# Ordering the loads of q, k and v behind earlier transposes in the DMA queue of a fused attention and mixture-of-experts kernel

## The chip, the cores and the metric

The kernel runs on one core of a Trainium2 chip. The metric is the device time of one launch in microseconds. The core has five engines that run their own instruction streams in order: TensorE (PE, with its weight loads PEld), VectorE (DVE), ScalarE (ACT), GpSimd (POOL) and SyncE (SP). SyncE computes nothing here; it issues nearly all DMAs, one after the other.

## The reference, cut to what matters

Bucketed attention (a query sees the keys whose six sign bits equal its own), then a two-layer feed-forward net, then a mixture of eight experts, of which each token uses two.

```python
q_bits = (einsum('bhsd,dk->bhsk', q, proj) > 0); k_bits = ...   # batch 2, heads 8, seq 768, dim 64
mask = q_bucket[:, :, :, None] == k_bucket[:, :, None, :]
scores = where(mask, scale * q @ k.T, -1e9)
attn_out = softmax(scores) @ v
x = attn_out as [1536, 512]
h = x @ w_in;  x = (h * sigmoid(1.702 * h)) @ w_out              # d_ff 2048
...
out[mask] += top2_w[mask, k, None] * (relu(x[mask] @ w1[e]) @ w2[e])   # 8 experts, top 2
```

## The kernel before

Everything is computed with pairs of half-precision numbers (a high and a low part), so a float32 input is loaded, converted, split and laid out before TensorE can use it.

**The steps.** The attention runs in 96 steps g: batch b, chunk cc of 256 queries, pair of heads hp, head h and half t. A step makes the scores (`qk`, L254), the row maximum (`rowmax`, L266 on VectorE), the exponential (`expo`, L275 on ScalarE), its split (`e_hi` L314, `e_lo` L321 or L323), and from step 16 on a DMA transpose of the result (`et<-er`, L327). `pv` (L368) multiplies with v after two heads. Before step 0 there are 17 steps with negative numbers, in which the first tiles are made ready. From step 20 on the first feed-forward net runs in between, chunk by chunk (`moe_pe`: L460 and L471; L478, L490, L504, L505 around them), and the routing of its tokens. After step 100 come the rest of that net and the experts (L799, L821).

**The preparation of q and k.** `load` (L118) issues the load of a q tile (128 KB) or a k or v tile (192 KB). A tile goes through `stack_hi` two steps later (L144 on VectorE or GpSimd, L145 on GpSimd, L151), `stack_lo` (L158 on ScalarE and then the transpose L169), `buckets` and `one_hot` (L179 to L203) and `stack_end` (L210 on ScalarE and then the transpose L211). Loads of k and v share four buffers (tag x32); a buffer is free when the tile in it has been split, for v by `v_hi` (L230, L231 on ScalarE) and `v_lo` (L237 on GpSimd). v tiles of the first 16 steps take another way (`v_load32`, L221).

**The weights of the first net.** `w_load` (L417) loads 32 blocks of 512 KB into three buffers; `w_bits` makes three passes over a block on VectorE (L428, L431, L434), `w_split` scales and splits it on ScalarE and GpSimd (L444 or L442, L445, L446). A buffer is free after L446.

**What sets the order.** The program hands over each step's calls in lists (`at` late in the step, `soon` and `start` earlier), and tables say in which step a tile is loaded, two steps ahead of `stack_hi`. For steps below 100 (`GM=100`) the order is not the program's: a scheduler lays the instructions out engine by engine, by its own model of time, and may put an instruction far ahead of its step as soon as its inputs and its buffer are free in that model. A load has no inputs. From step 100 on the written order holds. On the chip every engine, SyncE too, takes its instructions strictly in the order that results.

Of the kernel before, what the change touches and what calls it, by code (L numbers as in the profile page):

```python
# [60 lines left out]
def fused(ctx: ExitStack, tc: tile.TileContext, q, k, v, proj, w_in, w_out, w_gate, w_noise, noise,  # L61
          w1, w2, out, dbg=None):
    nc = tc.nc
# [48 lines left out]


    raw, rows, kts, qts, vts, bks = {}, {}, {}, {}, {}, {}
    FL = "p h c d -> p (h c) d"


    def load(nm, b, u):  # L118
        hp, i = u
        if nm == "q":  # L120
            x = att.tile([128, 2, CT, D], F32, name="q32")
            PARAM['LE'](nc).dma_start(x.rearrange("p h c d -> p h (c d)"), q[b, 2 * hp:2 * hp + 2].rearrange(
                "h (p c) d -> p h (c d)", c=NT)[:, :, i * CT * D:(i + 1) * CT * D])
        else:
            x = att.tile([128, 1, NT, D], F32, name=f"{nm}32", tag="x32", bufs=4)
            PARAM['LE'](nc).dma_start(x[:, 0].rearrange("p c d -> p (c d)"), (k if nm == "k" else v)[b, 2 * hp + i].rearrange(
                "(p c) d -> p (c d)", c=NT))
        raw[nm, b, u] = x

    def stack_hi(nm, b, u):  # L130
# [10 lines left out]
        h0 = 0 if nm == "q" else 64  # L141
        hi = sb[:, :, :, 0:64].rearrange(FL)
        eng = nc.gpsimd if PARAM["HE"](nm, b) == "P" else nc.vector
        eng.tensor_scalar(hi, x.rearrange(FL), GX, GX, op0=OP.add, op1=OP.subtract)  # L144
        nc.gpsimd.tensor_tensor(x.rearrange(FL), x.rearrange(FL), hi, op=OP.subtract)  # L145
        yield
        m, o = PARAM["SC"](nm, b), sa[:, :, :, h0:h0 + 64].rearrange(FL)
        if m == "A":
# [4 lines left out]
    def stack_lo(nm, b, u):  # L153
        x = raw.pop((nm, b, u))
        sa, sb = rows[nm, b, u]
        hp, i = u
        h0 = 64 if nm == "q" else 0
        nc.scalar.activation(sa[:, :, :, h0:h0 + 64].rearrange(FL), x.rearrange(FL), AF.Copy, scale=SH)  # L158
        if nm == "q":
            xt = att.tile([128, 2, 2, CT, 128], F16, name="qt", bufs=3)  # L160
            qts[b, hp, i] = xt
        elif i == 0:
            xt = att.tile([128, 2, 2, NT, 128], F16, name="kt", bufs=4)
            kts[b, hp] = xt
        else:
            xt = kts[b, hp]
        dst = xt if nm == "q" else xt[:, :, i:i + 1]
        rows[nm, b, u] = sb, dst
        nc.sync.dma_start_transpose(dst[:, 0].rearrange("p h c t -> p (h c) t"), sa.rearrange("p h c d -> p (h c d)"))  # L169

    def buckets(nm, b, u):
        sb, xt = rows[nm, b, u]
# [33 lines left out]
    def stack_end(nm, b, u):  # L206
        sb, xt = rows.pop((nm, b, u))
        oh = sb[:, :, :, 64:].rearrange(FL)
        if PARAM["OE"](nm, b) == "D":
            nc.scalar.activation(oh, oh, AF.Identity, scale=BIG, bias=-BIG if nm == "k" else 0.0)  # L210
        nc.sync.dma_start_transpose(xt[:, 1].rearrange("p h c t -> p (h c) t"), sb.rearrange("p h c d -> p (h c d)"))  # L211

    FU = PARAM["FU"]
    vfs = {}
# [25 lines left out]
    st, ets, xts, pos, sms = {}, {}, {}, {}, {}  # L240
# [75 lines left out]
    def e_lo(g):  # L316
        b, cc, hp, h, t = where(g)
        d = st.pop(g)
        er = d["er"]
        if g < NG:  # L320
            (nc.gpsimd if PARAM["LO"](g) else nc.vector).tensor_tensor(er[:, 1], d["e"], er[:, 0], op=OP.subtract)  # L321
        else:
            nc.vector.scalar_tensor_tensor(er[:, 1], d["e"], d["mx"][:, 3:4], er[:, 0], op0=OP.mult, op1=OP.subtract)  # L323
        if t == 0:
            et = att.tile([128, 2 * NT, CT, 128], F16, name="et", bufs=3)
            ets[b, cc, hp, h] = et
        nc.sync.dma_start_transpose(ets[b, cc, hp, h][:, :, t, :], er.rearrange("p s c -> p (s c)"))  # L327

    def early_unit(b, cc, hp):
        return (b * NCH + cc) * 16 + 4 * hp < NG  # L330
# [556 lines left out]
    for b in range(B):  # L887
        for hp in range(HP):
            g = b * NCH * 16 + 4 * hp
# [9 lines left out]
        for cc in range(NCH):  # L899
            for hp in range(HP):  # L900
                g = (b * NCH + cc) * 16 + 4 * hp
# [56 lines left out]
    order = ExitStack()  # L958
    g_lo = min(todo)
    for g in range(g_lo, G1 + 1):  # L960
        if g == max(PARAM["GM"], g_lo):
            order.enter_context(tc.manual_schedule(engines={
                mybir.EngineType.PE, mybir.EngineType.DVE, mybir.EngineType.Activation,
                mybir.EngineType.Pool, mybir.EngineType.SP}))
        if g == NU + 3:
            att_ctx.close()
            m2 = ctx.enter_context(tc.tile_pool(name="m2", bufs=2))
        prev = steps.get(g - 1, [])
        if 0 <= g + 2 < NU:
            qk(g + 2)  # L970
        for f, a in early.pop(g, []):
            f(*a)
        for x in prev:
            moe_act(*x)
        if 0 <= g + 1 < NU:
            rowmax(g + 1)
            expo(g + 1)
            e_hi(g + 1)
        for f, a in first.pop(g, []):
            f(*a)  # L980
        for x in prev:
            moe_dve(*x)
        if 0 <= g < FU:
            e_turn(g)
            e_copy(g)
        elif FU <= g < NU:
            e_lo(g)
        for x in steps.get(g, []):
            moe_pe(*x)
        for x in prev:  # L990
            moe_split(*x)
        by_turns(todo.pop(g, []))
# [52 lines left out]
    with tc.If(most > CAP):  # L1045
        with tc.tile_pool(name="ov", bufs=1) as ov:
# [13 lines left out]
            with tc.For_i(0, E, 1) as e:  # L1060
# [5 lines left out]
                with tc.If(here > CAP):  # L1066
# [12 lines left out]
                    with tc.For_i(0, (OV + 127) // 128, 1) as k_:  # L1079
                        with tc.If(here > k_ * 128 + CAP):  # L1080
# [11 lines left out]
                            xt = rowt.bitcast(F16)  # L1092
# [59 lines left out]
```

## Time and profile before

| | us |
|---|---|
| median of 3 runs (823.86 to 825.7) | 825.37 |
| the profiled execution | 823.72 |
| its span, first to last instruction | 822.0 |
| TensorE busy | 715.9 (87%) |
| VectorE busy | 533.9 (65%) |
| ScalarE busy | 445.0 (54%) |
| GpSimd busy | 267.9 (33%) |

A share over the whole span says little here, since the stages have different limits: the tables of busy time by stretch, the list of waits of an engine and the timeline of SyncE's queue say more. In such a list a wait is put down to what ended last. L12 means line 12 of the kernel; tile names stand as written<-read.

### The profile page before, as it was taken

How to read it: one execution, taken by the hardware profiler on the slowest of the kernel's cores; microseconds unless marked ns; L12 is line 12 of the kernel's file. 1: busy time of each engine (PE TensorE's matmuls, PEld its weight loads, DVE VectorE, ACT ScalarE, POOL GpSimd, SP SyncE). 2: the span in 40 equal slices, each digit the busy share in tenths (PEclk: the TensorE clock that was granted, in tenths of full speed). 3: DMA queues.
4: the chain of work that ended last, by engine and by line, in shares of the span. 5: the costliest groups of instructions: out<-in, count | busy, mean ns of one | idle time of the engine just before them, and what ended most of it. 6: DMA issues, size and time to landing. Idle time of an engine off the chain costs nothing.

```text
span 822.0 us, 14816 instructions
## 1 busy us (share of the span) xinstructions
PE 715.9 (87%) x5398; PEld 446.0 (54%) x5399; DVE 533.9 (65%) x1330; ACT 445.0 (54%) x859; POOL 267.9 (33%) x303
## 2 busy tenths in 40 slices
PE   1676478988988888898999999879999999999995
PEld 1343345646754665466568576547554655556553
DVE  8998799997896789569869526454633525345210
ACT  3778767766765686467567425234533534334220
POOL 6444646560444055314212132241021120311212
PEclk9878789999999999999999999999999999999998
DMA  8999689999999999995797542856875858677213
GB/s 218 224 251 212 180 187 184 255 277 218 175 171 195 154 200 192 225 159 106 119 176 123 102 156 88 221 146 180 250 158 173 199 111 232 135 194 176 28 19 47
DMA packets 268126, 140.04 MB, mean 170 GB/s; under 512 B 224720, under 2 KB 243856, under 8 KB 268048
## 3 DMA queue, kind: packets, MB, share of 16 engines
q1 hardware_dynamic: 261520, 125.37, 68.1%
q0 software_dynamic: 6528, 13.68, 9.3%
q8 instruction: 43, 0.70, 0.4%
q14 instruction: 35, 0.29, 0.1%
HBM read 61.48 MB, written 23.79 MB: 104 GB/s over the span
## 4 chain that ended last, share of the span: by engine, by line
PE 42%; DVE 5%; DMA 3%; POOL 2%; issue 1%; ACT 1%; POOLq 0%; ACTq 0%; DVEq 0%
PE ph L799 15%; PE py L821 13%; PE px L471 6%; PE h L460 3%; PE py L825 2%; DVE er L323 1%; DMA xg<-slots 1%; PE pv L368 1%; POOL slots L685 1%; DMA slots<-xr,si 1%; DMA et<-er 1%; PE s L254 1%; ACT er L314 1%; DVE e L266 1%; DVE th L490 1%
## 5 line engine op out<-in xcount | busy, mean ns | idle before, releaser
L460 PE MATMUL h<-xt,wi 128*128 128x256 f16 x1152 | 140.2, 277 | 6.2 <-DVE mx L279 3.2
L799 PE MATMUL ph<-xg,ew 128*128 128x400 f16 (+2 forms) x864 | 135.4, 320 | 8.9 <-DMA xg<-slots 8.4
L743 DVE SCALAR_TENSOR_TENSOR ew<-w,ew 128x1024 f16<-128x1024 f32 x64 | 77.9, 1226 | 88.2 <-ACT ew L742 88.0
L471 PE MATMUL px<-wo,gt 128*128 128x512 f16 x576 | 132.6, 382 | 0.5 <-DVE th L490 0.4
L460 PEld LDWEIGHTS <-wi 128*128 128x128 f16 x1152 | 112.5, 99 | 28.2 <-issue 9.1
L821 PE MATMUL py<-ew,ht 128*128 128x512 f16 x576 | 125.8, 379 | 0.0
L838 POOL DMA_INDIRECT out_dram<-yo,ti x32 | 51.2, 1600 | 216.7 <-ACT yo L835 216.7
L254 PE MATMUL s<-kt,qt 128*128 128x512 f16 (+1 forms) x384 | 88.2, 353 | 33.3 <-DVE mx L266 28.5
L799 PEld LDWEIGHTS <-ew 128*128 128x128 f16 x864 | 82.6, 100 | 59.8 <-issue 6.8
L275 ACT ACTIVATE e<-e,mx 128x768 f32<-128x768 f32 x96 | 89.4, 931 | 27.9 <-DVE mx L266 21.5
L505 POOL TENSOR_TENSOR gt<-th,gt 128x512 f16<-128x512 f32 x48 | 60.1, 1252 | 122.0 <-ACT gt L504 121.6
L266 DVE CUSTOM_DVE_ANT_0 e<-s,zero 128x768 f32<-128x768 f32 x96 | 90.6, 948 | 4.4 <-PE s L254 1.5
L821 PEld LDWEIGHTS <-ht 128*128 128x128 f16 x576 | 56.3, 98 | 67.0
L471 PEld LDWEIGHTS <-gt 128*128 128x128 f16 x576 | 55.3, 98 | 64.1 <-issue 3.2
L323 DVE SCALAR_TENSOR_TENSOR er<-e,mx,er 128x768 f16<-128x768 f32 x68 | 73.1, 1080 | 25.9 <-ACT er L314 25.3
L314 ACT ACTIVATE er<-e,mx 128x768 f16<-128x768 f32 x68 | 63.0, 930 | 37.8 <-DMA et<-er 21.6
L835 ACT ACTIVATE yo<-py,wv 128x512 f32<-128x512 f32 (+1 forms) x32 | 20.3, 633 | 102.4 <-PE py L821 54.6
L809 ACT ACTIVATE ht<-ph 128x400 f16<-128x400 f32 (+2 forms) x72 | 33.5, 466 | 73.0 <-PE ph L799 72.9
L254 PEld LDWEIGHTS <-qt 128*128 128x128 f16 x384 | 37.0, 103 | 62.7 <-issue 38.5
L810 DVE SCALAR_TENSOR_TENSOR ht<-ph,ht 128x400 f16<-128x400 f32 (+2 forms) x72 | 37.6, 524 | 49.5 <-ACT ht L809 49.5
L742 ACT ACTIVATE ew<-w 128x1024 f16<-128x1024 f32 x64 | 66.3, 1047 | 2.6 <-DMA w<-in_moe_w_dram 2.6
L368 PE MATMUL pv<-et,vt 128*64 128x256 f16 x720 | 51.2, 284 | 7.5 <-DMA et<-er 7.5
(195 smaller groups left out, 945.8 us busy)
## 6 DMA issues: line engine op xcount, KB each, us to landing
w<-in_moe_w_dram SPq DMA_DIRECT2D x64, 512.0 KB, 4.6
wraw<-in_moe_w_in_dram SPq DMA_DIRECT2D x16, 512.0 KB, 4.6
wraw<-in_moe_w_out_dram SPq DMA_DIRECT2D x16, 512.0 KB, 4.3
slots<-blank SPq DMA_DIRECT2D x6, 1032.0 KB, 6.8
v<-in_v_dram SPq DMA_DIRECT2D x24, 192.0 KB, 4.1
out_dram<-zeros SPq DMA_DIRECT2D x13, 256.0 KB, 3.4
k<-in_k_dram SPq DMA_DIRECT2D x16, 192.0 KB, 3.6
q<-in_q_dram SPq DMA_DIRECT2D x24, 128.0 KB, 3.1
```

Of the source, the lines that this page charges most:

```text
L254: nc.tensor.matmul(ps[:, n0 * 128:n1 * 128], qt[:, s, h, t, :], kt[:, s, h, n0:n1, :].rearrange("p c t -> p (c t)"), start=(s == 0), stop= ...
L266: nc.vector.tensor_tensor_reduce(e32, st[g]["ps"][:, :S], zero.to_broadcast([128, S]), -0.125, TOP, op0=OP.add, op1=OP.min, accum_out=mx[: ...
L275: nc.scalar.activation(e32, e32, AF.Exp, scale=-1.0, bias=st[g]["mx"][:, 1:2], accum_out=sms[b, cc, hp][:, 2 * h + t:2 * h + t + 1] if g < ...
L314: nc.scalar.activation(er[:, 0], st[g]["e"], AF.Copy, scale=r)
L323: nc.vector.scalar_tensor_tensor(er[:, 1], d["e"], d["mx"][:, 3:4], er[:, 0], op0=OP.mult, op1=OP.subtract)
L460: nc.tensor.matmul(ph[:, a, :], wi[ws][:, d, f0:f0 + 128], xt[:, d, xs, :], start=(d == 0 and ws == 0 and xs == 0), stop=(d == HP - 1 and ...
L471: nc.tensor.matmul(px, gts[ci, f // 2][:, gs, f % 2, t * 128:t * 128 + 128], wo[ws][:, f, :], start=(f == 0 and gs == 0 and ws == 0), stop ...
L505: nc.gpsimd.tensor_tensor(gt[:, 1], th, gt[:, 0], op=OP.subtract)
L742: nc.scalar.activation(hi, x, AF.Copy, scale=SW1 if j == 0 else SW2)
L743: nc.vector.scalar_tensor_tensor(lo, x, SW1 if j == 0 else SW2, hi, op0=OP.mult, op1=OP.subtract)
L799: nc.tensor.matmul(ph[:, :c1 - c0], w[:, ws, d * FE + f * 128:d * FE + f * 128 + 128], xg[e, p][:, xs * HP + d, :], start=(d == 0 and ws = ...
L821: nc.tensor.matmul(py, ht[:, f, hs, t * 128:t * 128 + 128], w[:, ws, f * DM:(f + 1) * DM], start=(i == 0), stop=(i == n - 1))
```

## The change

`load` becomes a wrapper. The program now notes the step that it is writing (`now[0] = g`) and, for each step, the last DMA transpose that it has written in it (`spq`; transposes L169, L211 and L327 are noted, those of the routing are not). A load is then written with an edge to the latest noted transpose that stands at least five steps back: on SyncE's queue the load may not be put ahead of it. This is an order in the queue alone, no wait for the transpose's data. Before the first transposes (written in step -14) no such edge exists. The loads of weights, of `v_load32` and all others have none.

```diff
+    now, spq = [0], {}
...
     def load(nm, b, u):
+        hp, i = u
+        behind = max((s for s in spq if s <= now[0] - 5), default=None)
+        with ExitStack() as es:
+            if behind is not None:
+                es.enter_context(tc.issue_after(spq[behind].ins))
+            load_(nm, b, u)
+
+    def load_(nm, b, u):
         hp, i = u
...
-        nc.sync.dma_start_transpose(dst[:, 0].rearrange("p h c t -> p (h c) t"), sa.rearrange("p h c d -> p (h c d)"))
+        spq[now[0]] = nc.sync.dma_start_transpose(dst[:, 0].rearrange("p h c t -> p (h c) t"), sa.rearrange("p h c d -> p (h c d)"))
...
     for g in range(g_lo, G1 + 1):
+        now[0] = g
```

The two other transposes are noted in the same way. The instructions stay the same in kind and number; the scheduler's order of all five engines differs up to about step 75. Line numbers of the changed kernel are higher by 10 or 11 from here on (L136 is the old L126, L213 the old L203, L427 the old L417). In the rows below, k32, q32 and v32 are the loaded tiles, wraw a block of weights, ks, qsa and qsb the stacks that are transposed into kt and qt.

SyncE's queue around the weight load wraw_900, some 75 rows into it, before:

```order
L126 DMA v32_1482<-in_v_dram 128x384
L126 DMA v32_1484<-in_v_dram 128x384
L417 DMA wraw_846<-in_moe_w_in_dram 128x1024
L211 DMA_TRANSPOSE qt_892<-qsb_864 128x4x128
L126 DMA v32_1892<-in_v_dram 128x384
L126 DMA v32_1956<-in_v_dram 128x384
L417 DMA wraw_900<-in_moe_w_out_dram 128x1024
L126 DMA k32_2368<-in_k_dram 128x384
L169 DMA_TRANSPOSE qt_1302<-qsa_1279 128x4x128
L122 DMA q32_1585<-in_q_dram 128x2x128
L126 DMA k32_2516<-in_k_dram 128x384
L417 DMA wraw_959<-in_moe_w_out_dram 128x1024
```

And the same place of the changed kernel:

```order
L427 DMA wraw_846<-in_moe_w_in_dram 128x1024
L231 DMA v32_1067<-in_v_dram 128x384
L136 DMA v32_1136<-in_v_dram 128x384
L179 DMA_TRANSPOSE qt_954<-qsa_933 128x4x128
L132 DMA q32_1193<-in_q_dram 128x2x128
L136 DMA v32_1223<-in_v_dram 128x384
L221 DMA_TRANSPOSE qt_892<-qsb_864 128x4x128
L427 DMA wraw_900<-in_moe_w_out_dram 128x1024
L427 DMA wraw_959<-in_moe_w_out_dram 128x1024
```

The four v loads 1482 to 1956 have moved behind the first et transposes, k32_2368 and k32_2516 some 60 rows further down, behind twenty of them.

SyncE's queue in the start, before:

```order
L417 DMA wraw0_208<-in_moe_w_in_dram 128x1024
L126 DMA k32_210<-in_k_dram 128x384
L126 DMA k32_212<-in_k_dram 128x384
L169 DMA_TRANSPOSE kt_163<-ks_153 128x6x128
L169 DMA_TRANSPOSE qt_166<-qsa_156 128x4x128
L417 DMA wraw0_214<-in_moe_w_in_dram 128x1024
L126 DMA k32_216<-in_k_dram 128x384
L417 DMA wraw_231<-in_moe_w_in_dram 128x1024
L122 DMA q32_233<-in_q_dram 128x2x128
L169 DMA_TRANSPOSE kt_163<-ks_218 128x6x128
```

And in the changed kernel, from the same load on:

```order
L427 DMA wraw0_208<-in_moe_w_in_dram 128x1024
L427 DMA wraw0_214<-in_moe_w_in_dram 128x1024
L427 DMA wraw_231<-in_moe_w_in_dram 128x1024
L179 DMA_TRANSPOSE kt_163<-ks_153 128x6x128
L179 DMA_TRANSPOSE qt_166<-qsa_156 128x4x128
L136 DMA k32_210<-in_k_dram 128x384
L136 DMA k32_212<-in_k_dram 128x384
```

Nine more loads follow there (of weights, of v for the first steps and of small inputs), and then, on the same queue:

```order
L179 DMA_TRANSPOSE kt_163<-ks_218 128x6x128
L221 DMA_TRANSPOSE kt_163<-ks_153 128x6x128
L221 DMA_TRANSPOSE qt_166<-qsb_157 128x4x128
L136 DMA k32_216<-in_k_dram 128x384
L132 DMA q32_233<-in_q_dram 128x2x128
```

The k loads have moved behind the first two transposes, k32_216 and q32_233 behind the transpose of the one-hot qsb_157, and weight loads have taken their places.

VectorE at the use of k32_216 (it makes ks_242), before:

```order
L191 TENSOR_TENSOR pc_181<-pc_181,pow2_89 128x6x6
L194 TENSOR_REDUCE bk_198<-pc_181 128x6
L203 TENSOR_TENSOR ks_153<-iota_i_78,bk_198 128x6x64
L428 TENSOR_SCALAR wf_245<-wraw0_214 128x512
L189 TENSOR_TENSOR pc_192<-pc_192 128x4x6
L144 TENSOR_SCALAR ks_242<-k32_216 128x6x64
```

And in the changed kernel, from the one-hot qsb_157, whose transpose stands ahead of the load of k32_216, to the use:

```order
L213 TENSOR_TENSOR qsb_157<-iota_i_78,bk_200 128x4x64
L438 TENSOR_SCALAR wf_418<-wraw_316 128x512
L441 SCALAR_TENSOR_TENSOR wf_418<-wraw_316,wf_418 128x512
L558 SCALAR_TENSOR_TENSOR wg_123<-wg32_122,wg_123 128x4x16
L444 SCALAR_TENSOR_TENSOR wraw_316<-wraw_316,wf_418 128x512
L199 TENSOR_TENSOR pc_263<-pc_263 128x6x6
L201 TENSOR_TENSOR pc_263<-pc_263,pow2_89 128x6x6
L204 TENSOR_REDUCE bk_284<-pc_263 128x6
L213 TENSOR_TENSOR ks_218<-iota_i_78,bk_284 128x6x64
L154 TENSOR_SCALAR ks_242<-k32_216 128x6x64
```

The use has moved back behind the one-hot of another tile and a block of weights; before, the load stood ahead of that one-hot's transpose.

## Rows read from the trace of the kernel before

**Rows 1.** Busy time by stretch: stretch, its us, busy (instructions) per engine, clock, DMA.

```profile
0.00:25.00 25.00, 5.19 (x72) 3.47 (x74) 21.79 (x61) 9.17 (x22) 15.35 (x52) 1.00 0.79 198
...
75.00:100.00 25.00, 12.58 (x89) 7.51 (x88) 17.73 (x37) 19.49 (x47) 15.46 (x15) 0.86 0.66 160
...
150.00:175.00 25.00, 21.26 (x161) 12.67 (x160) 24.97 (x48) 17.00 (x32) 14.84 (x13) 1.00 1.11 285
...
200.00:225.00 25.00, 22.14 (x261) 17.93 (x259) 22.02 (x60) 19.90 (x45) 9.88 (x9) 1.00 1.01 177
...
450.00:475.00 25.00, 25.00 (x191) 14.56 (x190) 13.25 (x49) 10.46 (x24) 3.82 (x4) 1.00 0.68 126
```

**Rows 2.** VectorE's waits at 75 to 100 us: us in total, times, longest.

```profile
DVE wf L428 <- DMA wraw<-in_moe_w_out_dram: 4.1, 2, 2.8
DVE wf L428 <- DMA wraw<-in_moe_w_in_dram: 2.4, 1, 2.4
```

**Rows 3.** SyncE's timeline at 70 to 100 us: start, us taken, what.

```profile
71.64 1.02 SPq L126 DMA_DIRECT2D v<-in_v_dram  x2
76.31 0.33 SPq L417 DMA_DIRECT2D wraw<-in_moe_w_in_dram  x1
...
78.40 7.13 SPq L126 DMA_DIRECT2D v<-in_v_dram  x2
86.78 0.33 SPq L417 DMA_DIRECT2D wraw<-in_moe_w_out_dram  x1
```

**Rows 4.** SyncE's waits at 50 to 100 us.

```profile
SPq L126 <- POOL vt L237: 8.9, 4, 6.2
SPq L417 <- POOL wi L446: 6.4, 4, 3.6
```

**Rows 5.** ScalarE's groups at 70 to 95 us: count, busy us, mean ns, idle before.

```profile
L230 ACT ACTIVATE v<-v 128x384 f32<-128x384 f32 x6 | 3.0, 526 | 1.4 <-DMA v<-in_v_dram 1.4
```

**Rows 6.** VectorE's groups over the span, and one timeline row of L548.

```profile
L434 DVE SCALAR_TENSOR_TENSOR wraw<-wraw,wf 128x512 int32<-128x512 int32 x32 | 29.2, 913 | 0.4
L431 DVE SCALAR_TENSOR_TENSOR wf<-wraw,wf 128x512 int32<-128x512 int32 x32 | 26.0, 811 | 0.1
L428 DVE TENSOR_SCALAR wf<-wraw 128x512 int32<-128x512 int32 x32 | 16.5, 516 | 6.8 <-DMA wraw<-in_moe_w_out_dram 4.1 <-DMA wraw<-in_moe_w_in_dram 2.7
L191 DVE TENSOR_TENSOR pc<-pc,pow 128x24 f32<-128x24 f32 (+1 forms) x40 | 16.1, 403 | 0.2
...
L203 DVE TENSOR_TENSOR ks<-iota_i,bk 128x384 f16<-128x384 f16 x16 | 10.2, 639 | 0.1
...
L189 DVE TENSOR_TENSOR pc<-pc 128x24 f32<-128x24 f32 (+1 forms) x40 | 9.3, 233 | 0.1
L203 DVE TENSOR_TENSOR qsb<-iota_i,bk 128x256 f16<-128x256 f16 x12 | 9.1, 754 | 0.0
...
L194 DVE TENSOR_REDUCE bk<-pc 128x4 f32<-128x24 f32 (+1 forms) x40 | 7.0, 175 | 0.2
...
47.21 0.94 DVE L548 SCALAR_TENSOR_TENSOR wg<-wg,wg 128x64 f16<-128x64 f32 x1
```

**Rows 7.** First 50 us: timeline of one pass to a load, and DMA flights.

```profile
18.37 0.40 ACT L210 ACTIVATE qsb<-qsb 128x256 f16<-128x256 f16 x1
...
19.25 1.21 SPq L211 DMA_TRANSPOSE qt<-qsb  x1
...
24.70 0.42 SPq L126 DMA_DIRECT2D k<-in_k_dram  x1
...
wraw<-in_moe_w_in_dram SPq DMA_DIRECT2D x10, 512.0 KB, 4.4
k<-in_k_dram SPq DMA_DIRECT2D x8, 192.0 KB, 4.0
```

**Rows 8.** DMA at 200 to 250 us: queue (packets, MB, share), one issue (KB, us).

```profile
q1 hardware_dynamic: 30371, 8.67, 98.5%
...
k<-in_k_dram SPq DMA_DIRECT2D x3, 192.0 KB, 3.2
```

More of the change, by code (lines that the diff above doesn't have):

```diff
@@ L210, in stack_end @@
             nc.scalar.activation(oh, oh, AF.Identity, scale=BIG, bias=-BIG if nm == "k" else 0.0)
-        nc.sync.dma_start_transpose(xt[:, 1].rearrange("p h c t -> p (h c) t"), sb.rearrange("p h c d -> p (h c d)"))
+        spq[now[0]] = nc.sync.dma_start_transpose(xt[:, 1].rearrange("p h c t -> p (h c) t"), sb.rearrange("p h c d -> p (h c d)"))
     FU = PARAM["FU"]
@@ L326, in e_lo @@
             ets[b, cc, hp, h] = et
-        nc.sync.dma_start_transpose(ets[b, cc, hp, h][:, :, t, :], er.rearrange("p s c -> p (s c)"))
+        spq[now[0]] = nc.sync.dma_start_transpose(ets[b, cc, hp, h][:, :, t, :], er.rearrange("p s c -> p (s c)"))
     def early_unit(b, cc, hp):
```

## The prediction

> **What bounds the kernel now.** I read the busy times by stretch of 25 us first [rows 1]. From about 400 us to the end TensorE is busy nearly all the time (25.00 of 25.00 us at 450 to 475), and the change moves no instruction there; that end moves only if the work before it arrives earlier or later. Before that, two limits follow each other. In the first 175 us VectorE is the fullest engine (21.79 of the first 25 us, 24.97 of 25 at 150 to 175), except in one stretch, 75 to 100 us, where it is busy for 17.73 us only. From 200 us TensorE is at 22 of 25 us, VectorE as well, and the two wait for each other in turn.
>
> So the question for a change in SyncE's queue is the hole in VectorE at 75 to 100 us. The list of VectorE's waits in that stretch says what ends them [rows 2]: three times L428, the first pass over a block of the MoE weights (tile wraw), waits for the load of that block, 4.1 + 2.4 = 6.5 us. A load is late because its issue was late, so SyncE's own timeline is next [rows 3]. A pair of v loads (L126) occupies the queue from 78.40 for 7.13 us, and the weight load behind it goes out at 86.78; the one before went out at 76.31, though the instruction ahead of it, another pair of v loads, was through at 72.66. SyncE's waits between 50 and 100 us name both reasons [rows 4]: the v loads wait 8.9 us for GpSimd's L237, which frees the buffer of an earlier v tile (four buffers for k and v together), and the weight loads wait 6.4 us for GpSimd's L446, which frees one of their three. SyncE issues in order: what stands behind a waiting v load waits too, needed or not.
>
> **What the change removes.** The order of the built program shows it: v32_1892 and v32_1956, which stood right ahead of the weight load wraw_900, now stand behind the sixth et transpose and later, and the four k loads for batch 1, which were strewn between the weight loads, stand some 60 rows further down. Of all these early loads the weight loads wraw_900 and wraw_959 then have only v32_1136 and v32_1223 ahead of them, which take the buffers of k tiles from the start. The two waits of 4.1 us hang on the blocked stretch directly. The third, 2.4 us, hangs on the buffer that L446 frees late; ScalarE feeds L446, and between 70 and 95 us it spends 3.0 us on six L230 [rows 5] and as much on the L231 that follow each, for v tiles that were loaded early. In the new order of ScalarE these v steps stand some 20 to 37 us of work later, so that wait should go as well. Bounds: 4.1 and 6.5 us; I take 6.5, because both of its causes move away.
>
> **What the change adds.** A load that is issued late can itself be late. For each of the 26 q and k loads that VectorE converts and that lie behind a transpose I took VectorE's work between the instruction that feeds the last transpose ahead of the load and the instruction that uses the load, each at the mean of its group. The shortest is k32_216 in the start: between the one-hot for qsb_157 (L203 in the old numbering) and the use stand L428, L431, L548, L434, L189, L191, L194 and L203. With the one-hot itself that is 0.75 + 0.52 + 0.81 + 0.94 + 0.91 + 0.23 + 0.40 + 0.18 + 0.64 = 5.4 us [rows 6]. What has to fit into it: the one-hot 0.75, ScalarE's L210 0.40, the issue of the transpose 1.21, the issue of the load 0.42 and its flight of 4.0, 6.8 us together [rows 6, 7]. VectorE would wait 1.4 us there. By the same count the next three (k32_2368, q32_1585, q32_233) have 5.5 to 6.7 us, and the other 22 have 8.1 us or more and wait for nothing. With 6.8 us for all, the second costs 1.3 us and the others up to 0.5 together; but for k32_2368 the flight is 3.2 us, not 4.0 [rows 8], so 0.5 us is nearer, and q32_233 sits in the shadow of the wait just before it. Sum: 1.4 + 0.5 + 0.4 = 2.3, I take 2.5 us. Bounds: 0 (flights as short as 3 us), and 16 us if the way from one-hot to landed load takes 9 us instead of 6.8.
>
> What it moves costs nothing in the sum, with these covers. In the start three weight loads now go ahead of the first transposes instead of one and two k loads, 640 KB more in the same queue; VectorE has the three passes over those blocks to do meanwhile (0.52 + 0.81 + 0.91 us each [rows 6], 6.7 us for three), so the transposes may land some 2 us later. Without that cover it would cost those 2 us. Work on VectorE is neither added nor taken: weighed by group means, 4.8 us less stand ahead of the row maximum of step 16, 0.3 us more ahead of that of step 40, and the same at step 64, so this gain is lent and paid back. The four k loads of 192 KB move from an idle DMA time into 200 to 250 us, where the queue is busy for 98.5% [rows 8]. If the DMA engines were the limit there, 0.79 MB at the 173 GB/s of that stretch (8.67 MB in 50 us) would cost 4.5 us; I take 0, because a k load flies 3.2 us there, less than the 4.0 of the start, so the queue still has room; 4.5 stays for the range. Last, the changed order of MoE and attention matmuls between 100 and 330 us can shift a few us either way; I put 4 us on both sides.
>
> **A rule against it.** The two rows that speak are the hole at 75 to 100 us and the 4.0 us flight. The Trainium skill, "Trainium Kernel Development and Optimization", Best Practices, says to double-buffer so that DMA overlaps compute; by it, taking the head start from 26 loads can only lose, and the second rival below is what that would look like. The Trainium skill, "DMA: Bandwidth & Descriptors", Anatomy of one DMA, fits a DMA (of the GpSimd path) at 2.0 us plus its bytes over 436 GB/s; 192 KB would then take an estimated 2.45 us, the added waits would be gone and the sum would be the first rival's. The row has 4.0 us and decides.
>
> **The sum.** -6.5 + 2.5 = -4.0 us, on the profiled execution's 823.72 us (its span of 822.0 and 1.7 around it): 819.7. The median of the three runs shown is 825.37, 1.65 above that execution, so against it the same difference gives **821.4 us**. A difference under 0.2%, 1.65 us, can't be told from no change in this kernel.
>
> **Rivals.**
> *All gain.* The loads fly in 3 us and nothing waits for them, and ScalarE, rid of early v work, feeds the weights sooner: -6.5 us, 818.9, with luck in the reordered middle 814. For it: SyncE's queue is emptier. Against: flights of 4.0 us in the first 50 us [rows 7].
> *Late loads, slower.* Place: the conversions of k and q on VectorE (L144), in order, with the row maxima behind them. If the way from one-hot to landed load takes 7.5 us, the waits add up to 6.0 us and eat the gain (a break-even at about 7.6); at 8.5 us they are 11.3, +4.8 us net, 830.2. For it: in the built program each DMA waits for the one eight before it, weight loads fly 4.4 us [rows 7], and in the start eleven loads now stand between the first two transposes and the third. Against: wherever the loads were not early already (batch 1, q), GpSimd and not VectorE paid for it.
> *Gain absorbed.* VectorE is earlier at 100 us, but TensorE at 22 of 25 us [rows 1] and the waits between the two take it back by 390 us: 825.4.
> That the change doesn't do what it says is excluded by the built order, except for the first loads, which have no transpose ahead of them.
>
> **How the numbers follow.** Forecast (a gain of 2 to 6 us) 0.45, all gain 0.13, absorbed 0.15, slower 0.27. Faster by over 0.2% is the first two, 0.58; within 0.2% 0.15; slower 0.27. The forecast's own range is 817.5 to 825. The range for 8 in 10 goes from 814.5 (all gain with half of the 4 us for order) to 830.5 (late loads at 8.5 us); beyond it lie about 0.1 on the slow side and less on the other.
>
> **What would show it.** Right: VectorE busy for more than 22 us at 75 to 100 us, no wait of L428 for wraw over 1 us, short waits of L144 for k in the start and near 200 us. Wrong: L144 waits for k or q that add up to more than 6 us; waits of L428 that stay (then GpSimd's L446, not the v loads, held the weight loads); or row maxima that come earlier at step 16 and not at step 72.

## The result, and the profile after

| | before | after |
|---|---|---|
| median, us (4 runs each) | 824.62 (823.68 to 825.70) | 832.89 (831.50 to 833.97) |
| the profiled execution, us | 823.72 | 832.14 |
| its span | 822.0 | 830.4 |
| VectorE busy | 533.9 | 540.7 |
| GpSimd busy | 267.9 | 271.2 |

The ratio is 1.0091, with a 95% interval of 1.0075 to 1.0108: the changed kernel is slower by 8.3 us, where 4.0 us faster was forecast. Below 460 us the change does two things, one after the other. The busy times by stretch of the changed kernel (PE, PEld, DVE, ACT, POOL, each with its count; then the granted clock, the DMA share, GB/s) show the first:

```profile
0.00:25.00 25.00, 2.62 (x36) 1.69 (x37) 21.76 (x56) 9.17 (x20) 14.65 (x51) 1.00 0.74 206
25.00:50.00 25.00, 16.13 (x114) 9.73 (x116) 22.26 (x55) 16.31 (x38) 11.88 (x11) 0.81 0.92 208
50.00:75.00 25.00, 18.21 (x170) 11.79 (x167) 21.86 (x61) 21.86 (x54) 9.49 (x10) 0.92 0.78 195
75.00:100.00 25.00, 17.95 (x122) 10.13 (x122) 23.47 (x54) 20.52 (x48) 12.00 (x13) 0.83 0.82 203
150.00:175.00 25.00, 20.33 (x131) 11.38 (x132) 24.86 (x43) 14.90 (x27) 14.77 (x12) 0.93 0.96 252
```

The hole of [rows 1] is filled: VectorE is busy for 23.47 us at 75 to 100 us, where it was 17.73. The row maximum of step 16 comes earlier. These are the timeline rows (start, length) of that row maximum, and of the one of step 72, first in the kernel before:

```profile
99.67 0.94 DVE L266 CUSTOM_DVE_ANT_0 e<-s,zero 128x768 f32<-128x768 f32 x1
...
365.97 0.95 DVE L266 CUSTOM_DVE_ANT_0 e<-s,zero 128x768 f32<-128x768 f32 x1
```

and then in the changed one:

```profile
92.06 0.94 DVE L276 CUSTOM_DVE_ANT_0 e<-s,zero 128x768 f32<-128x768 f32 x1
...
372.96 0.94 DVE L276 CUSTOM_DVE_ANT_0 e<-s,zero 128x768 f32<-128x768 f32 x1
```

So 7.6 us ahead at step 16, and 7.0 us behind at step 72: 14.6 us are lost between 100 and 370 us. Most of that is lost by 250 us. The stretch from 100 to 250 us, first of the kernel before, then of the changed one:

```profile
100.00:250.00 150.00, 128.38 (x1088) 85.89 (x1088) 136.61 (x320) 108.98 (x218) 70.17 (x61) 0.94 0.99 209
```

```profile
100.00:250.00 150.00, 122.67 (x1002) 81.10 (x1000) 135.07 (x282) 101.78 (x201) 72.31 (x61) 0.95 0.92 204
```

VectorE is as busy as before (135.07 and 136.61 of 150 us), but it gets through 282 instructions instead of 320. It hardly waits longer (14.93 us idle and 13.39); its instructions last longer. The groups of the changed kernel that answer to [rows 6] (count, busy us, mean ns, idle before) say which ones:

```profile
L441 DVE SCALAR_TENSOR_TENSOR wf<-wraw,wf 128x512 int32<-128x512 int32 x32 | 28.9, 905 | 0.3
L444 DVE SCALAR_TENSOR_TENSOR wraw<-wraw,wf 128x512 int32<-128x512 int32 x32 | 27.3, 854 | 0.3
L438 DVE TENSOR_SCALAR wf<-wraw 128x512 int32<-128x512 int32 x32 | 21.1, 660 | 1.1 <-DMA wraw<-in_moe_w_in_dram 1.0
L201 DVE TENSOR_TENSOR pc<-pc,pow 128x24 f32<-128x24 f32 (+1 forms) x40 | 17.8, 446 | 0.1
L199 DVE TENSOR_TENSOR pc<-pc 128x24 f32<-128x24 f32 (+1 forms) x40 | 15.9, 398 | 0.6 <-ACT pc L194 0.6
```

The same 32 first passes over a weight block (L438, the old L428) took 516 ns each and now take 660; the 40 comparisons of L199 (L189) took 233 and take 398. The work in them hasn't changed. What lengthens them is seen when VectorE's and GpSimd's timelines are laid side by side. VectorE of the changed kernel at 112 us:

```profile
112.87 1.66 DVE L441 SCALAR_TENSOR_TENSOR wf<-wraw,wf 128x512 int32<-128x512 int32 x1
114.45 1.61 DVE L348 TENSOR_SCALAR sm<-sm 128x4 f32<-128x4 f32 x1
115.98 0.69 DVE L444 SCALAR_TENSOR_TENSOR wraw<-wraw,wf 128x512 int32<-128x512 int32 x1
...
118.63 1.36 DVE L438 TENSOR_SCALAR wf<-wraw 128x512 int32<-128x512 int32 x1
```

and GpSimd there:

```profile
112.83 1.15 POOL L456 TENSOR_TENSOR wo<-wraw,wo 128x512 f16<-128x512 f32 x1
113.94 2.09 POOL L331 TENSOR_TENSOR er<-e,er 128x768 f16<-128x768 f32 x1
...
118.56 1.15 POOL L456 TENSOR_TENSOR wo<-wraw,wo 128x512 f16<-128x512 f32 x1
```

L348 works on four columns and takes 0.16 us elsewhere. Here it starts at 114.45, half a microsecond into GpSimd's L331, and ends at 116.06, 0.03 us after L331 does (116.03). L441 starts 0.04 us after a GpSimd L456 and ends 0.55 us after it, most of its own 0.68. So a VectorE instruction that starts while a GpSimd subtraction runs can wait inside itself until that has ended. No list of waits shows this, since the instruction counts as busy.

Ahead of the row maximum of step 72, 206 VectorE instructions of the kernel before started while a GpSimd subtraction (a TENSOR_TENSOR) ran; 74 of them were longer than their undisturbed length (the 20% point of their form) by over 0.2 us, by 54.9 us together. In the changed kernel it is 224, 83 and 61.3 us. Of those that had no GpSimd instruction beside them at all (404 and 393), and of those that were already running when one began (101 and 88), none was. The row maxima, which read the scores from PSUM, had GpSimd beside them in some 100 of L266's 192 instructions and lost 0.5 us in all.

The Trainium skill, "SBUF — State Buffer", Who interferes with whom, states the rule: VectorE and GpSimd share one pair of ports, which VectorE needs in its two-port modes and, against a GpSimd instruction that reads SBUF, for an instruction with two SBUF inputs; whoever issues first holds it for the whole instruction and the other is blocked. The trace agrees for GpSimd's subtractions, with the numbers just given; beside GpSimd's L144 it shows almost no blocking (1 instruction of 20, last section).

From here on the time of a row maximum is split into three parts. For each form of VectorE's instructions the undisturbed length is that of its shortest fifth (L428 0.42 us, L191 0.18, L189 0.17). **Work** is the sum of the undisturbed lengths ahead of that row maximum (less the 0.1 us by which neighbours overlap, so that it wanders by a few us), **excess** what the instructions lasted beyond them (the overlap is off here too, so a lengthening under 0.1 us passes for work), **waits** the rest. In the kernel before, step 72 at 366.0 us is 257 of work, 53.5 of excess and 55.5 of waits. The changed kernel against it:

| at step | time | work | excess | waits |
|---|---|---|---|---|
| 16 | -7.6 | -2.4 | -3.8 | -1.4 |
| 32 | +4.3 | +0.2 | +5.6 | -1.4 |
| 72 | +7.0 | +1.1 | +7.3 | -1.4 |

The waits did fall, and kept what they had gained. The excess more than ate it. VectorE's busy time on the page, 533.9 and 540.7 us for the same 1330 instructions, says the same: +6.8.

The last 1.4 us come mostly after 520 us, where TensorE waits for the second expert's tokens, 3.77 us before and 4.16 after, and then runs 24 matmuls at a low clock. This is the row of the kernel before, and the one of the changed kernel:

```profile
525.76 4.35 PE L799 MATMUL ph<-xg,ew 128*128 128x256 f16 x24 [3.77 <-DMA xg<-slots]
```

```profile
532.97 5.30 PE L809 MATMUL ph<-xg,ew 128*128 128x256 f16 x24 [4.16 <-DMA xg<-slots]
```

The granted clock is 0.66 in the 5 us from 526 before, and 0.51 in the 6 us from 533 after.

### The profile page after: what moved, and what is told of

It is laid out like the page before. It is cut to its first block, busy times and chain, and to the rows that moved or that the text cites. A ratio compares the mean times of both kernels' runs of the same rounds, so it can differ in the third digit from the quotient of the medians.

```text
span 830.4 us, 14807 instructions
## 1 busy us (share of the span) xinstructions
PE 715.4 (86%) x5398; PEld 444.1 (53%) x5399; DVE 540.7 (65%) x1330; ACT 446.6 (54%) x859; POOL 271.2 (33%) x303
## 4 chain that ended last, share of the span: by engine, by line
PE 43%; DVE 25%; DMA 15%; issue 7%; ACT 5%; SPq 2%; POOL 2%; POOLq 0%; DVEq 0%; ACTq 0%
PE ph L809 15%; PE py L831 13%; DMA et<-er 5%; PE h L470 5%; DVE er L333 4%; DVE e L276 4%; PE px L481 3%; PE py L835 2%; DMA kt<-ks 2%; ACT er L324 2%; DVE wf L441 2%; DMA slots<-xr,si 2%; DVE th L500 2%; DMA qt<-qsb 1%; POOL slots L695 1%
## 5 line engine op out<-in xcount | busy, mean ns | idle before, releaser
L470 PE MATMUL h<-xt,wi 128*128 128x256 f16 x1152 | 142.9, 280 | 11.2 <-DVE th L500 8.9
L470 PEld LDWEIGHTS <-wi 128*128 128x128 f16 x1152 | 113.7, 100 | 35.9 <-issue 13.9
```

What stands on the lines that cost most here:

```text
L470: nc.tensor.matmul(ph[:, a, :], wi[ws][:, d, f0:f0 + 128], xt[:, d, xs, :], start=(d == 0 and ws == 0 and xs == 0), stop=(d == HP - 1 and ...
```

## The experiments

The theories: **lock** (the loss is the excess; it hangs on which instructions of VectorE and GpSimd fall beside each other, and so on the order of the engines) and **late loads** (the prediction's second rival: q and k loads that land late). All are compared with the kernel before on the same chip. The columns: ratio of the times with its interval, and at step 72 the difference in time, excess and waits from the kernel before, in the profiled execution (what the sum lacks is work). The kernel before has one trace, the one that was read above.

| run | ratio | time | excess | waits |
|---|---|---|---|---|
| changed kernel | 1.0091 (1.0075 to 1.0108) | +7.0 | +7.3 | -1.4 |
| order_only | 1.0100 (1.0079 to 1.0122) | +10.5 | +4.8 | +4.6 |
| v_only | 1.0019 (0.9998 to 1.0040) | +4.6 | +4.1 | -0.7 |
| kq_only | 1.0083 (1.0064 to 1.0102) | +11.5 | +6.7 | +3.5 |
| from0 | 1.0036 (1.0019 to 1.0053) | +5.4 | +5.1 | -0.5 |
| d10 | 1.0066 (1.0041 to 1.0090) | +6.0 | +4.9 | +1.6 |
| d20 | 1.0054 (1.0028 to 1.0080) | +1.4 | +1.2 | -0.7 |
| one_k | 1.0072 (1.0045 to 1.0099) | +3.0 | +3.0 | -1.1 |
| one_v | 1.0019 (1.0000 to 1.0038) | +3.3 | -1.2 | +3.4 |
| sp_swap | 1.0021 (0.9998 to 1.0044) | +0.4 | -2.3 | +2.5 |
| both_swap | 1.0017 (0.9996 to 1.0038) | +1.4 | -2.5 | +3.8 |
| split_before | 0.9974 (0.9958 to 0.9990) | +1.8 | -12.1 | +10.4 |
| split_after | 1.0013 (0.9996 to 1.0030) | +3.3 | -11.3 | +10.0 |
| split_v | 0.9956 (0.9941 to 0.9972) | -3.8 | -8.7 | +0.1 |
| split_wvx | 0.9981 (0.9961 to 1.0002) | -2.3 | -9.0 | +3.1 |

A profile is of one execution. Those of split_before (830.54 us, its median 823.85), kq_only (839.06 and 834.09), d10 (831.69 and 828.94) and one_v (828.77 and 826.17) were the longest of their kernels, those of d20 (826.08 and 828.09) and split_v (820.49 and 821.65) the shortest, so the last three columns of a single run are rough. In the runs with halves many lengthenings are under 0.1 us: split_before has the order of the kernel before, so its work can't differ, and yet its columns leave 3.5 us for it. With every lengthening counted, the excess at step 72 is 9.4, 8.4, 5.3 and 6.1 us below the kernel before in the last four rows, and 8.2 above it in the changed kernel.

### The order without the edges

The program is built twice. The first build has the edges and gives the order of four engines; the second has no edges, but is held to that order:

```diff
-    with _tile.TileContext(nc, schedule_with_timeline_sim=True) as tc:
-        fused(tc, *args)
...
+    EDGES[0] = True
+    nc, arrays = build(None)
+    order = {e: n for e, n in engine_order(nc).items() if not e.endswith("SP")}
+    EDGES[0] = False
+    nc, arrays = build(order)
```

> The edges are undone, but TensorE, VectorE, ScalarE and GpSimd keep the order that the changed kernel has; only SyncE's queue is laid out anew, with the q, k and v loads free to go early. Lock theory (the loss is VectorE instructions that last longer because they start while a GpSimd instruction runs; that hangs on the order of the compute engines, not on when a load lands): VectorE's waits between 25 and 75 us shrink by 2 to 4 us, the long VectorE instructions stay some 5 to 8 us above those of the kernel before, and the time is 828 to 833. Late-load rival (the loss is q and k loads that land late): the loads are early again, the loss goes, 818 to 826.

It took 835.24 us. Loads that are free to go early don't bring the time back; the late-load theory had at most 826. The time is also above the lock theory's 833, the excess at its lower bound (4.8, where 5 to 8 were expected), and VectorE's waits at 25 to 75 us, which were to shrink by 2 to 4 us, grew. Its list of them (what waited for what: us in total, times, longest) has no load of q or k any more and begins with

```profile
DVE e L295 <- PE s L283: 5.0, 3, 2.8
```

The scores themselves wait for transposes (6.6 us for qt<-qsb on TensorE in that stretch). That the early loads hold these transposes up in the queue is likely but not shown. For the order that the changed kernel has, the edges themselves show no cost.

### The edge for some of the loads

Three kernels with one more condition each on the edge, `nm == "v"`, `nm != "v"` and `now[0] >= 0`:

```diff
-        behind = max((s for s in spq if s <= now[0] - 5), default=None)
+        behind = max((s for s in spq if s <= now[0] - 5 and nm == "v"), default=None)
```

> Only loads of v get the edge. Late-load rival: the gain at 75 to 100 us without late q and k loads, 817 to 820. Lock theory: VectorE's waits fall by some 6 us at 75 to 100 us here too, but the order of all engines is a new one, so the long VectorE instructions change by several us in a direction that nobody can say; at step 72 the difference from the kernel before is the sum of less waiting and that change, 815 to 830.

> Only loads of q and k get the edge, those of v stay as early as before. Late-load rival: the waits of the late loads without the gain at 75 to 100 us, so slower than the changed kernel or equal to it, 831 to 840. Lock theory: VectorE's waits are 2 to 5 us above the kernel before, and the long VectorE instructions again change by several us either way: 820 to 838, with the time at step 72 following the sum.

> The edge only for loads written from step 0 on; the 17 steps ahead of it are left as before. Late-load rival: the 4 us of waits of VectorE between 25 and 75 us go, the rest stays, 827 to 829. Lock theory: those waits go as well, but the long VectorE instructions are drawn anew: 815 to 832, and not tied to 828.

The medians were 827.85, 834.09 and 828.58 us. kq_only and from0 fall where late loads put them, v_only does not (817 to 820). v_only has 2.5 us less of waits at step 16 and is 4.9 us ahead there, but at step 72 it is 4.6 us behind, of which 4.1 are excess. Two smaller expectations failed: VectorE's idle time at 75 to 100 us falls by 3.6 us in v_only, not by 6, and at 25 to 75 us it is still 4.0 us in from0 (5.88 in the changed kernel, 1.46 before). The lock theory's ranges were so wide that these three alone decide little; what they show is that the excess rose in every one.

### Fewer edges

The distance ten or twenty in place of five, and the edge for one load alone, by `(nm, b, u) == ("k", 1, (0, 0))` or `("v", 0, (3, 1))` in the same condition.

> The edge goes to a transpose ten or more steps back in place of five. The start up to the load of wraw_900 keeps the order before; v32_1892, v32_1956 and the four k loads for batch 1 move back. This is what the prediction credited with -6.5 us, without the late loads of the start. If the delay itself brings GpSimd's work beside VectorE's, VectorE's excess over its undisturbed lengths at step 72 is near that of the changed kernel (+5 to +8 us against before) and the time 825 to 828. If the excess is a matter of chance with each new order, it lies anywhere between -3 and +8 us, and the time follows: 817 to 830.

> Twenty steps in place of five: only a few k loads for batch 1 move back, and less far. If the delay itself makes the excess, it is below that of ten steps, +0 to +3 us at step 72, and the time within 2 us of before. If it is chance, it is as large as in the others, +2 to +8 us or below zero, and the time 820 to 832.

> The edge for one load alone, k32_2368, the first k tile of batch 1. One late load of 192 KB can cost 1 us at most at its use; a fifth of VectorE's instructions below step 100 stand in another place all the same. Delay theory: excess within 1.5 us of before, time 824 to 827. Chance theory: excess at step 72 off by 2 to 8 us, time 820 to 832.

> The edge for one load alone, v32_1956, one of the two that stood ahead of wraw_900. Delay theory: excess within 1.5 us of before; with ScalarE rid of that tile's work at 75 to 100 us a gain of 0 to 3 us, 822 to 826. Chance theory: excess at step 72 off by 2 to 8 us, time 818 to 832.

They took 828.94, 828.09, 829.39 and 826.17 us. d10 leaves the start as it was and moves mainly what the prediction credited with 6.5 us (v32_1892, v32_1956, the k loads); it is slower by 0.66%, with 4.9 us of excess. One load that is put further back (one_k) costs 0.72%; in its trace 460 of VectorE's first 990 places hold another instruction than in the kernel before, and only about half of the cost, 3.0 us, is there at step 72. Neither side of this test came out whole: the excess is 3.0 us up in one_k, where delay alone allowed 1.5, and 1.2 down in one_v, where chance wanted 2 to 8; d20 has the small excess that delay alone allowed (1.2) but not its time (3.6 us above the kernel before, where 2 were allowed). The kernels with many edges have 4 to 7 us of excess, those with few -1 to 3. None of the eight orders that came out of these edges (the changed kernel's among them) is faster than the order before; six are slower beyond their intervals, v_only and one_v by 0.19% with intervals that touch no change. Whether the excess grows with the number of delayed loads or by chance isn't settled, nor why the order before is better than all eight.

### GpSimd's subtractions cut short

This is the strongest test. Both kernels keep their own order on all five engines, and nearly all of GpSimd's subtractions work on 16 columns:

```diff
+    def less(dst, x, hi, cut=True):
+        if not (CUT[0] and cut):
+            nc.gpsimd.tensor_tensor(dst, x, hi, op=OP.subtract)
+        else:
+            at_ = (slice(None),) + (0,) * (len(x.shape) - 2) + (slice(0, 16),)
+            nc.gpsimd.tensor_tensor(dst[at_], x[at_], hi[at_], op=OP.subtract)
```

> The kernel before, its order on all engines kept, with GpSimd's subtractions (low parts of q, k, v, of the weights, and of the gated values from the second chunk on) done on 16 columns only; what reads a low part of v, weights or gated values reads the high part in its place, so the low parts are left out of the result. Lock theory: VectorE's instructions lose most of the time they spend above their undisturbed length (61 us up to the last row maximum), to under 25 us, and the time falls by 10 to 45 us. If the long instructions have another cause than GpSimd, the 61 us stay.

> The changed kernel with the same cut and its own order kept. Lock theory: VectorE's excess falls to under 25 us here too, and against the cut kernel before, the row maximum of step 72 comes between 4 us earlier and 2 us later, where it was 7.0 us later uncut. Rivals (late loads, or the changed order of attention and feed-forward matmuls on TensorE): the difference at step 72 stays at 5 to 9 us.

The first pass over the weights, first of the cut kernel before, then of the cut changed kernel:

```profile
L464 DVE TENSOR_SCALAR wf<-wraw 128x512 int32<-128x512 int32 x32 | 14.3, 447 | 13.9 <-DMA wraw<-in_moe_w_in_dram 9.8 <-DMA wraw<-in_moe_w_out_dram 4.1
```

```profile
L464 DVE TENSOR_SCALAR wf<-wraw 128x512 int32<-128x512 int32 x32 | 15.3, 478 | 6.6 <-DMA wraw<-in_moe_w_in_dram 3.3 <-DMA wraw<-in_moe_w_out_dram 3.1
```

447 and 478 ns in place of 516 and 660. The excess up to the last row maximum falls from 61 us to 11 in the one and from 68 to 14 in the other. And the row maximum of step 72, again first before, then changed:

```profile
351.63 0.95 DVE L302 CUSTOM_DVE_ANT_0 e<-s,zero 128x768 f32<-128x768 f32 x1
```

```profile
346.34 0.95 DVE L302 CUSTOM_DVE_ANT_0 e<-s,zero 128x768 f32<-128x768 f32 x1
```

With GpSimd out of the way, the changed kernel is 5.3 us ahead at step 72, where it was 7.0 behind. That is 1.3 us beyond what the lock theory expected and far from the +5 to +9 of its rivals: without GpSimd's subtractions there is a gain, with them a loss. Not all of this swing of 12.3 us is excess, though. Between the two kernels the excess at step 72 differs by 2.8 us here, where it was 7.3, but the waits by -8.7, where it was -1.4: a VectorE that is held up less waits more for weights (13.9 us in the rows above, 6.8 uncut), and so their earlier loads bring more. The cut also shortens GpSimd's own way to the buffers that it frees, so it doesn't single out the meetings by itself; the count of lengthened instructions above does. The times of the whole, 922.18 and 923.03 us, are no guide. With other values an expert gets more than 400 tokens, and a branch runs that is skipped otherwise (5518 matmuls on the page in place of 5398).

### What held the weight load

The prediction said that two waiting v loads hold up wraw_900 in SyncE's queue. Here the order before is kept on all engines, but for one load on SyncE (sp_swap), or that and two subtractions on GpSimd (both_swap). In the code the instructions stand by their numbers; here by what they do:

```diff
+    for eng, ins, ahead_of in [("SP", wraw_900, v32_1892), ("Pool", L446 of wraw_739, L145 of q32_1193),
+                               ("Pool", L446 of wraw_789, L237 of v32_1482)]:
+        q = order["EngineType." + eng]
+        q.remove(ins)
+        q.insert(q.index(ahead_of), ins)
```

> The order before on all engines, but on SyncE the weight load wraw_900 stands ahead of the two v loads v32_1892 and v32_1956. By the prediction (the waiting v loads hold the weight load up): the first wait of 2.8 us for wraw_out at 75 to 100 us goes, and the time falls by 2 to 4 us to 821 to 823. Rival (the weight's own buffer is the last to come free, since the L446 that frees it ends at 86.74 us and the load goes out at 86.78): the wait stays and the time is the same within 1.5 us.

> As the run before, and on GpSimd the weight subtraction L446 for wraw_739 stands ahead of the subtraction L145 for q32_1193 (which waits for VectorE), the one for wraw_789 ahead of the two L237 that stood before it. Buffer theory: the load of wraw_900 goes out near 83.5 us in place of 86.8, VectorE's waits of 2.8 and 1.3 us for weights shrink to under 1 us together, and 2 to 4 us are gained at step 16; the time is 820.5 to 823 if VectorE's long instructions stay as they are, and up to 2 us off that if they shift. If instead only a new order brought the changed kernel its gain at 75 to 100 us, nothing changes: 824 to 826.

sp_swap took 825.93 us. The timeline of GpSimd and of SyncE in it:

```profile
85.36 1.60 POOL L475 TENSOR_TENSOR wi<-wraw,wi 128x512 f16<-128x512 f32 x1
```

```profile
86.99 0.33 SPq L446 DMA_DIRECT2D wraw<-in_moe_w_out_dram  x1
```

With no v load ahead of it, the weight load goes out at 86.99, as soon as the subtraction that frees its buffer ends (86.96). So it was GpSimd's place in the order that held it, not the v loads, and VectorE's first wait for it at 75 to 104 us is as long as before (2.8 us):

```profile
DVE wf L457 <- DMA wraw<-in_moe_w_out_dram: 4.6, 2, 2.8
```

both_swap took 826.00. Its load goes out 3.5 us earlier, as expected:

```profile
83.44 0.33 SPq L446 DMA_DIRECT2D wraw<-in_moe_w_out_dram  x1
```

but VectorE gains nothing, where 2 to 4 us were expected: its waits for weights shrink to 2.0 us, and another takes their place. VectorE's longest wait there at 75 to 104 us, and ScalarE's at 75 to 100 us:

```profile
DVE e L295 <- PE pt L322: 6.6, 2, 6.4
```

```profile
ACT v L259 <- DMA v<-in_v_dram: 3.6, 1, 3.6
```

The v loads, now behind the weight, come late for ScalarE, which converts them in its own fixed order ahead of what TensorE and VectorE need. The wait has moved.

### Halves

If one long GpSimd instruction is what VectorE waits for, two short ones should cost it less. Each subtraction is written as two, and each kernel keeps its own order:

```diff
-            nc.gpsimd.tensor_tensor(dst, x, hi, op=OP.subtract)
...
+        m = x.shape[1] // 2
+        nc.gpsimd.tensor_tensor(dst[:, :m], x[:, :m], hi[:, :m], op=OP.subtract)
+        nc.gpsimd.tensor_tensor(dst[:, m:], x[:, m:], hi[:, m:], op=OP.subtract)
```

> The kernel before, its order on all engines kept, each of GpSimd's subtractions for low parts (L145, L237, L446, L505) written as two instructions over half the columns each. By the lengths that the cut kernel showed (0.26 us for 16 columns against 1.25 for 512), a half takes some 0.75 us. Lock theory: a VectorE instruction that starts beside one waits for the end of a half and not of a whole, so VectorE's excess of 61 us up to the last row maximum falls by 12 to 25 us, part of which its waits take back; time 814 to 822, faster than before. If VectorE isn't let in between the halves, the excess stays and GpSimd's longer way costs 0 to 4 us: 824 to 829.

> The same halves in the changed kernel, with its own order. Lock theory: the excess of 68 us falls by 15 to 28 us, more than in the kernel before since there is more of it, and the difference between the two kernels shrinks from 8 us to between 0 and 5; time 816 to 825. If VectorE isn't let in between the halves: 831 to 837.

> The edge for loads of v alone, in that kernel's own order, with the subtractions in halves. Uncut it had 4.9 us less at step 16 and was 0.2% slower in the end. Lock theory: the halves take 3 to 7 us off, as in the two kernels before, 820 to 825; if so, a part of the change's gain is kept and this beats the kernel before. If the halves helped the other two by chance: 825 to 830.

> The kernel before in its order, with halves for the subtractions of q, k, v and the weights, but not for the gated values (L505), most of which fall after 200 us, where VectorE has waits anyway. Lock theory: the excess up to step 32 (177 us) falls nearly as far as with all halves, by 5 to 8 us, and GpSimd stays shorter afterwards; 821 to 825. If L505 made the difference, the gain goes: 825 to 827.

A half takes 0.73 us, as these groups of GpSimd in split_before show:

```profile
L139 POOL TENSOR_TENSOR gt<-th,gt 128x256 f16<-128x256 f32 x48 | 35.0, 729 | 116.9 <-ACT gt L542 115.7 <-issue 0.8
L140 POOL TENSOR_TENSOR gt<-th,gt 128x256 f16<-128x256 f32 x48 | 34.9, 726 | 0.0
```

so GpSimd is busy for 300.0 us in place of 267.9, and still the kernel before gains 0.26%, at 823.85 us. The changed kernel falls from 1.0091 to 1.0013 of the kernel before, at 826.26: most of its loss is gone with nothing else changed. With halves the distance between the two kernels is 0.39% in place of 0.91%. Both times miss what was expected: 823.85 us lies above 814 to 822 and 826.26 above 816 to 825. In split_before waits of VectorE take back all of the excess up to step 72 (+10.4 us of waits, in an execution that was its longest), so a microsecond less of excess isn't a microsecond less of time. The edge for v loads alone with halves (split_v) is the fastest, 821.65 us, 0.44% below the kernel before. Its stretch from 100 to 250 us has 311 instructions in 132.47 us, 426 ns each; the changed kernel had 479 (135.07 for 282), the kernel before 427:

```profile
100.00:250.00 150.00, 126.93 (x1072) 84.00 (x1069) 132.47 (x311) 110.59 (x220) 90.77 (x114) 0.95 1.01 217
```

Halves for the preparation alone (split_wvx) bring 0.19%, with an interval that just touches no change; its 822.96 us and the 821.65 of split_v lie in the lock theory's ranges.

## Why the prediction was wrong

**The bound and the place.** VectorE as the bound of the first 175 us, and the hole at 75 to 100 us as what the change can fill, were right: 23.47 us busy, more than the 22 named as the sign. The change filled it.

**The term removed, -6.5 us.** The waits for weights (L428, now L438; [rows 2, 6]) went from 6.8 us to 1.1 over the span, and VectorE's idle time at 75 to 100 us from 7.27 to 1.53, -5.7. The size was nearly right, the cause half so: sp_swap and both_swap show that the buffers of the weights, which GpSimd frees, held wraw_900, and that ScalarE's early v work matters with them. What the prediction held for the cause of the third wait only, the late L446 behind ScalarE's v work, was at work in the others too.

**The term added, +2.5 us.** VectorE's waits at 25 to 75 us for loads of q and k in the changed kernel are

```profile
DVE qsb L154 <- DMA q<-in_q_dram: 2.0, 2, 1.0
DVE ks L154 <- DMA k<-in_k_dram: 1.1, 1, 1.1
```

3.1 us together; a k tile in the start costs 1.1 us, where 1.4 was worked out. The flight of a k load in the first 50 us even fell, from 4.0 us [rows 7] to 2.9. Over the attention's steps the same two add up to 4.7 us, 1.0 of them there before, so +3.7. All waits of VectorE at 25 to 75 us, small ones too, rose by 4.4 us (5.88 idle in place of 1.46, at 24.43 and 24.11 us busy in the two stretches before). This is the term that was sized too low, by 1 to 2 us. The net of the waits is -1.4 us at step 16 and still at step 72, against -4.0 in the sum.

**The step that failed.** "Work on VectorE is neither added nor taken: weighed by group means" took each instruction at the mean of its group in the kernel before. That mean is no property of the instruction: the 516 ns of L428 are 0.42 us where GpSimd doesn't hold it and mostly 0.8 to 1.4 where it does. The change moved both engines' instructions and with them the number of those that GpSimd held up, 74 to 83 ahead of step 72. The term that was put at zero measured +7.3 us there. How much of it the kernel would keep if these meetings went and nothing else changed isn't shown: in split_before waits grew as the excess fell. The 4 us on both sides for the changed order were meant for TensorE's matmuls and were too few. That [rows 6] gave 754 ns for L203 on 256 columns and 639 on 384 was the sign that these means hold something else.

**The rivals.** "Late loads, slower" had the right side and almost the right time (830.2), by a mechanism that isn't the one: it reckoned with 11.3 us of waits for late q and k loads, 3.7 came, and order_only has the loads early and is no faster. That its time is close is luck. "Gain absorbed" named TensorE and the waits between the two; it was VectorE itself.

**The signs.** "Row maxima that come earlier at step 16 and not at step 72" was listed as what would show it wrong, and is what came. The signs of being right came as well (VectorE's busy time, no wait for weights over 0.7 us, k waits of 1.1 us in the start and 0.7 near 200 us): they look at the waits alone, and not at how long the instructions last.

**The range.** Its lower end, 814.5, doesn't follow from its own words: all gain (818.9) with half of the 4 us for order gives 816.9. The measured time lies beyond the other end, 830.5, and that end had been set by late loads.

## What to carry to other kernels

A mean duration in a profile can hold waiting: where the same form of instruction shows a range of lengths, look at what runs on GpSimd beside the long ones before moving either, and price a move by undisturbed lengths and meetings apart. In a scheduled kernel one edge re-lays several engines, so weigh a change by what the built order does to all of them, and expect no gain from a new order as such: of the eight tried here none was faster. Where GpSimd and VectorE are both busy, shorter GpSimd instructions can pay even if they add up to more time.

## What the runs showed of the hardware

- Of 510 VectorE instructions that started while a GpSimd subtraction ran, in the two kernels, 178 were longer by over 0.2 us. In 174 of them the end lagged that of the subtraction by a fixed time, their undisturbed length less 0.12 to 0.20 us. None of the 124 of L266 (row maxima) or the 19 TENSOR_REDUCE of L194 among the 510 was lengthened so.
- It goes both ways. GpSimd's L456 on 512 columns takes 1.15 us, and 1.60 where VectorE was first.
- GpSimd's L144 (a TENSOR_SCALAR from float32 to float16) held up almost nobody: of 20 VectorE instructions that started beside it in the two kernels, on lines that its subtractions lengthen, one was longer by over 0.2 us. The TENSOR_SCALAR L442 (float32 in place) held up 7 of 10. Why they differ isn't shown.
- The same 24 matmuls took 4.35 us at a granted clock of 0.66 (part of the stretch at 2.4 GHz) and 5.30 at 0.51 (nearly all of it at 1.2), after TensorE had stood idle for DMA for 3.77 and 4.16 us.
